# One kernel of recurrence, MLP and gated MLP: the first MLP group in whole float32, later groups and the spatial product in float16 parts

## The chip, the cores and the metric

One Trainium2 chip, and on it one core. The metric is the device time of one execution in microseconds, taken as the median of several runs. One execution was also recorded by the profiler, instruction by instruction.

## What is computed

A model of three layers on two sequences (B = 2) of 768 tokens (S) with 384 features (8 heads of 48). All inputs are float32.

```python
# recurrence, per batch and head: state is 48 x 48
for t in range(S):
    cur = outer(u * k[t], v[t])
    y[t] = r[t] @ (state + cur)
    state = w[t][:, None] * state + outer(k[t], v[t])
# MLP: x is 2 x 768 x 384
xn = (x - mean(x)) / sqrt(var(x) + 1e-6) * g_ln
x = x + maximum(xn @ w_ch1, 0) @ w_ch2          # 384 -> 1536 -> 384
# gated MLP
h = maximum(x @ w_in, 0)                        # 384 -> 1024
u, v = h[..., :512], h[..., 512:]
v_n = (v - mean(v)) / sqrt(var(v) + 1e-6)
v_s = einsum('ts,bsd->btd', w_spatial, v_n) + b_spatial[None, :, None]
out = (u * v_s) @ w_out                         # 512 -> 384
```

The four weight matrices w_ch1, w_ch2, w_in and w_out arrive as float64 (`np.random.randn` times a scale that keeps float64), and the chip has to turn them into float32 itself.

## The kernel before

**The work.** The recurrence runs in chunks of 128 tokens; with two sequences there are 12 chunks, numbered i = 2c + b. `prep(i)` makes the decay products of a chunk on VectorE (two scans and several elementwise products), `keys_t`, `scores`, `values` and `state` are its matmuls, `norm(i)` the layer norm, `turned(i)` the transpositions on TensorE whose results are copied into the feature-major rows `x2v` (the residual) and `xring_h`, `xring_l` (the normalised rows as a high and a low part). Two chunks, one of each sequence, make a group of 256 tokens: `moe1(g)` is the MLP of group g, g = 0 to 5. It has 12 slices f of the hidden width. `up(f)` multiplies with w_ch1's slice, ScalarE and VectorE make the hidden rows `hh` and `hl`, and `down(f)` multiplies these with w_ch2's slice and sums in PSUM. After slice 11 two VectorE steps add the sums to `x2v` (lines 913 and 914).

**Parts.** Each product is made of three: `mm3` multiplies high by high, high by low and low by high part, all in the 4-byte type float32r, and sums in PSUM. In the trace these matmuls read f32.

**Weights.** `convert` turns a piece of 128 x 384 (or 128 x 256) float64 words into the parts, in a staging buffer `raw` of which there are four: a transfer; `shift` on the low words and `rebias` on the high words (ScalarE, lines 554 and 548); `sign` (ScalarE, line 561), which writes the sign over as a float16 value; `merge` (VectorE, line 565), which joins both words; the high part (ScalarE, line 373); the low part (VectorE, line 376). There are 12 pieces of w_ch1, 12 of w_ch2, 12 of w_in and 4 of w_out. The spatial matrix arrives as float32 and is halved, negated and split in `wsp`.

**The last phase.** When all groups are done, `v_tile` makes and normalises v (12 tiles), `u_tile` u, `sp_tile` the spatial product (16 tiles of 18 matmuls of 384 columns), `o_tile` the output. `verdict` compares the variances and the decays with limits; if one is not met, the general but slow function `general` computes the result again.

**The order.** All steps are given to a planner with an engine, an assumed cost, a key, and the tiles that they read and write:

```python
add("T", 9 * cm(256), ku(g, f), mm_, r=[("w1h", f), ("w1l", f), *xr], w=[p])
```

`order` walks through time and gives each engine, whenever it is free, the ready step with the smallest key; what comes out is a fixed order for each engine, and each engine works through its queue in that order. Transfers (engine "D") all go through SyncE's queue. The keys come from the constants `PP`: `T0` and `H0` place chunks 0 and 1, `CV`, `CS` and `CW` the weight pieces, `M0` and `M0S` the slices of group 0, `P`, `US` and `AH` the later groups and their chunks. While TensorE would stand idle before the first `down`, the planner puts in dummy products of zeros (`pw`, 128 x 128 in float16).

## Time and profile before

| what | value |
|---|---|
| median of 3 runs | 393.56 us (391.05 to 395.06) |
| the profiled execution | 389.08 us |
| its span, first to last instruction | 387.4 us |
| TensorE busy | 375.5 us, 97% |
| VectorE busy | 253.4 us, 65% |
| ScalarE busy | 189.0 us, 49% |
| HBM | 31.90 MB read, 2.36 MB written |

A matmul's record lasts longer than the distance to the next one, because matmuls overlap, so busy TensorE says only that it doesn't stand still; what a matmul costs is read from the distance of starts, or from the chain of waits, which gives a row of matmuls its length and its count. Names of tiles are those of the program without buffer numbers; `free` holds the parts of v and of the gated rows, `misc` other rows of the last phase, `p` and `acc` are results in PSUM. Lines 373, 376, 379 and 382 are helpers that record for many callers.

### The profile page before, as it was taken

The page shows a single profiled execution, that of the slowest core. Times are in us where ns is not written, and L with a number is a line of the kernel's source. Part 1 is how long each engine was busy: PE and PEld are TensorE (multiplying, and loading weights), DVE is VectorE, ACT ScalarE, POOL GpSimd, SP SyncE. Part 2 cuts the span into 40 slices and gives each one's busy share as a digit, 9 for nine tenths or more (in the row PEclk, how much of TensorE's full clock was granted, in tenths as well). Part 3 has the DMA queues.
Part 4 walks back from the last instruction along what each step waited for, and adds up shares of the span by engine and source line. Part 5 has one row for each costly group of instructions (what it writes and reads, how often), then busy time and mean ns, then how long its engine had stood idle before and what let it go on. Part 6 is the DMA issues. An engine that isn't in the chain of part 4 may idle for free.

```text
span 387.4 us, 7615 instructions
## 1 busy us (share of the span) xinstructions
PE 375.5 (97%) x3101; PEld 363.0 (94%) x3101; DVE 253.4 (65%) x598; ACT 189.0 (49%) x412; POOL 7.4 (2%) x21
## 2 busy tenths in 40 slices
PE   7899999999999999999999999999999999999994
...
GB/s 222 296 243 187 237 136 287 126 185 80 67 126 135 99 188 56 63 25 38 2 0 138 70 41 2 0 119 167 2 2 3 0 0 3 41 83 0 2 63 68
DMA packets 16092, 34.83 MB, mean 90 GB/s; under 512 B 1840, under 2 KB 8496, under 8 KB 16048
## 3 DMA queue, kind: packets, MB, share of 16 engines
...
HBM read 31.90 MB, written 2.36 MB: 88 GB/s over the span
## 4 chain that ended last, share of the span: by engine, by line
PE 80%; ACT 13%; DMA 4%; DVE 1%; SPq 0%; issue 0%; ACTq 0%
PE p L382 32%; PE acc L382 18%; ACT raw L561 5%; DMA raw<-in_w 3%; PE sc L382 2%; ACT raw L554 2%; ACT raw L548 2%; DMA dt<-in_dt 1%; ACT w1h L373 1%; ACT w2h L373 1%; PE y__2940 L382 1%; PE y__2762 L382 1%; PE y__1395 L382 1%; PE y__2277 L382 1%; PE y__2493 L382 1%; PE y__1978 L382 1%
## 5 line engine op out<-in xcount | busy, mean ns | idle before, releaser
L382 PE MATMUL acc<-hh,w2h 128*128 128x256 f32 x216 | 63.6, 295 | 0.0
L382 PE MATMUL acc<-hl,w2h 128*128 128x256 f32 x216 | 61.4, 284 | 0.5 <-DVE hl L883 0.4
L382 PE MATMUL acc<-hh,w2l 128*128 128x256 f32 x216 | 61.1, 283 | 0.0
L382 PE MATMUL p<-wsph,free 128*128 128x384 f32 x192 | 49.1, 335 | 0.0
L382 PEld LDWEIGHTS acc<-hl,w2h 128*128 128x128 f32 x216 | 41.3, 191 | 1.1 <-DVE hl L883 1.0
L382 PEld LDWEIGHTS acc<-hh,w2h 128*128 128x128 f32 x216 | 41.3, 191 | 0.8 <-ACT hh L879 0.2
L382 PEld LDWEIGHTS acc<-hh,w2l 128*128 128x128 f32 x216 | 41.2, 191 | 0.0
L561 ACT ACTIVATE raw<-raw 128x384 f16<-128x384 f32 (+1 forms) x40 | 39.4, 985 | 0.3
L382 PEld LDWEIGHTS p<-wsph,free 128*128 128x128 f32 x192 | 34.7, 188 | 0.1
L382 PE MATMUL p<-wspl,free 128*128 128x384 f32 x96 | 32.1, 334 | 0.0
L373 ACT ACTIVATE free<-misc 128x384 fp32r<-128x384 f32 x16 | 8.4, 525 | 44.3 <-DVE misc L1104 44.3
L1103 DVE TENSOR_TENSOR misc<-p,misc 128x384 f32<-128x384 f32 x16 | 8.9, 558 | 32.2 <-PE p L382 32.2
L382 PE MATMUL pw<-warm 128*128 128x128 f16 x367 | 25.8, 238 | 1.1 <-DVE warm L483 1.1
L565 DVE SCALAR_TENSOR_TENSOR raw<-raw 128x384 int32<-128x384 int32 (+1 forms) x40 | 20.5, 516 | 8.7 <-ACT raw L561 8.0
L382 PEld LDWEIGHTS <-warm 128*128 128x128 f16 x367 | 24.9, 110 | 1.3 <-DVE warm L483 1.1
L554 ACT ACTIVATE raw<-raw 128x384 uint32<-128x384 uint32 (+1 forms) x39 | 20.8, 534 | 10.6 <-DMA raw<-in_w 9.3
L548 ACT ACTIVATE raw<-raw 128x384 f32<-128x384 f32 (+1 forms) x40 | 21.0, 525 | 0.0
L382 PEld LDWEIGHTS p<-wspl,free 128*128 128x128 f32 x96 | 18.0, 188 | 0.0
L731 DVE TENSOR_TENSOR am<-sc,mask 128x512 f32<-128x512 f32 x24 | 15.7, 683 | 3.2 <-PE sc L382 3.2
L604 DVE TENSOR_TENSOR_SCAN Gs<-dt,onehot 112x516 f32<-112x516 f32 x12 | 14.7, 1226 | 3.4 <-DMA dt<-in_dt 3.4
L382 PE MATMUL p<-wol,free 128*128 128x384 f32 x48 | 16.2, 338 | 0.0
L382 PE MATMUL p<-woh,free 128*128 128x384 f32 x48 | 16.2, 337 | 0.0
...
## 6 DMA issues: line engine op xcount, KB each, us to landing
...
```

Of the source, the lines that this page charges most:

```text
L373: A.activation(out=out, in_=in_, func=ACTF.Copy)
L382: T.matmul(out=out, lhsT=lhsT, rhs=rhs, start=start, stop=stop)
L548: A.activation(out=e, in_=e, func=ACTF.Copy, scale=REBIAS)
L554: A.activation(out=z, in_=z, func=ACTF.Copy, scale=TOP3, bias=TOP3_BIAS)
L561: A.activation(out=z, in_=words()[0].bitcast(F32), func=ACTF.Copy)
L565: V.scalar_tensor_tensor(out=lw, in0=hw, scalar=3, in1=lw, op0=ALU.logical_shift_left, op1=ALU.bitwise_or)
L604: V.tensor_tensor_scan(out=g[:, n:0:-1], data0=d_()[:, 2 * NP * C + n:2 * NP * C:-1], data1=onehot[:, n:0:-1], initial=0.0, op0=ALU.mult, ...
L731: V.tensor_tensor(out=z, in0=t["sc", i][j].rearrange("q (h c) -> q h c", c=C), in1=mask.unsqueeze(1).to_broadcast([128, 4, C]), op=ALU.mult)
L1103: add("V", cv(384), key, lambda: V.tensor_tensor(out=tm_(), in0=t["spp", b, th, f][:, 0:384], in1=t["b"][:, ts], op=ALU.add), r=[p, "misc" ...
```

## The change

Group 0 of the MLP now works on whole float32 values: `merge` writes the joined word into new tiles `w1f` and `w2f`, the normalised rows of chunks 0 and 1 go to a new tile `xfirst`, and each product is one matmul, not three. A staging buffer is free after `merge`. The high and low parts of w_ch1 and w_ch2 are made later from `w1f` and `w2f`, by steps with keys of their own (`HK`, `HS`, `HW`), in float16; groups 1 to 5 take them, with normalised and hidden rows in float16 parts as well. The weights are scaled up by 2^8 on the way, and the sum after slice 11 is scaled back. The spatial product is made of float16 parts too, its matrix scaled by 2^15. `sign` is now a VectorE step for all four matrices: for 19 of the 24 MLP pieces a two-input operation, for 5 of them (letter U in `SG`) a 16-bit operation. Five shifts are on VectorE, before it was one. The steps that GpSimd did (some products of `prep`, some low parts) are on VectorE. `verdict` has range guards: maxima of the parts in float16, of g and of the spatial matrix, sums of `x2v`, and a least variance. Tiles are placed anew: the spatial matrix takes the place of `w1f`, the normalised v that of `w2f`, the high part of the gated rows that of `w1h` and `w1l`, w_out that of `w2h` and `w2l`. The constants `PP` and some assumed costs are new.

```diff
...
-PP = {'T0': 58.954, 'P': 31.457, 'H': 11.551, 'H0': 18.137, 'M0': 114.218, 'M0S': 6.6, 'AH': 31.444, 'AG': -14.296, 'US': 2.5, 'EV': 28.0, 'CV': -3.791, 'CS': 19.292, 'CW': 11.582, 'WK': 741.261, 'WS': -9.174, 'XK': 737.912, 'XS': 13.966, 'KG': 85.937, 'KU': 91.539, 'OK': 603.983, 'OS': 18.495, 'FG': 108.0, 'LOOK': 0.0, 'EK': 'V', 'EU': 'VVVGVVVVGV', 'ER': 'VVVVVGVVVVGV', 'RK': 'V', 'ED': 'V', 'SM': 'V', 'LO': 'V', 'SH': 'AAAAAAAVA', 'LW': 'GVVVVGV', 'LX': 'V', 'LS': 'V', 'LV': 'V', 'LU': 'GV'}
+PP = {'SK': 502.544, 'SS': -11.067, 'RG': 379.453, 'HK': 187.663, 'HS': 3.248, 'HW': 14.159, 'SG': 'VVVVVVVUVVVUVVVUVVVUVVVU', 'T0': 7.677, 'P': 40.921, 'H': 8.033, 'H0': 75.364, 'M0': 3.891, 'M0S': 17.135, 'AH': 39.301, 'AG': -60.723, 'US': 3.526, 'EV': 49.336, 'CV': 9.586, 'CS': 4.689, 'CW': 6.934, 'WK': 646.957, 'WS': 46.232, 'XK': 79.483, 'XS': 17.828, 'KG': 58.216, 'KU': 364.837, 'OK': 542.591, 'OS': 25.632, 'FG': 108.0, 'LOOK': 0.0, 'EK': 'V', 'EU': 'V', 'ER': 'V', 'RK': 'V', 'ED': 'V', 'SM': 'V', 'SH': 'AAAVAAVAAAAAAAAAAAAAVAV', 'LW': 'V', 'LX': 'V', 'LS': 'V', 'LV': 'V', 'LU': 'V'}
...
-    w1h = wpool.tile([128, KD, DH], F32R, tag="wa", name="w1h")
-    w1l = wpool.tile([128, KD, DH], F32R, tag="wb", name="w1l")
-    w2h = wpool.tile([128, KH, DM], F32R, tag="wc", name="w2h")
-    w2l = wpool.tile([128, KH, DM], F32R, tag="wd", name="w2l")
+    k_max = const.tile([128, 10], F32, name="k_max")
+    k_sum = const.tile([128, NCH], F32, name="k_sum")
+    w1f = wpool.tile([128, KD, DH], F32, tag="w1f", name="w1f")
+    w2f = wpool.tile([128, KH, DM], F32, tag="w2f", name="w2f")
+    w1h = wpool.tile([128, KD, DH], F16, tag="w1h", name="w1h")
+    w1l = wpool.tile([128, KD, DH], F16, tag="w1l", name="w1l")
+    w2h = wpool.tile([128, KH, DM], F16, tag="w2h", name="w2h")
+    w2l = wpool.tile([128, KH, DM], F16, tag="w2l", name="w2l")
     x2v = wpool.tile([128, KD, B * S], F32, tag="we", name="x2v")
-    xring_h = ring.tile([128, KD, RING * C], F32R, tag="xh", name="xring_h")
-    xring_l = ring.tile([128, KD, RING * C], F32R, tag="xl", name="xring_l")
+    xring_h = ring.tile([128, KD, RING * C], F16, tag="xh", name="xring_h")
+    xring_l = ring.tile([128, KD, RING * C], F16, tag="xl", name="xring_l")
+    xfirst = ring.tile([128, KD, B * C], F32, tag="xf", name="xfirst")
...
-            A.activation(out=e, in_=e, func=ACTF.Copy, scale=REBIAS)
+            A.activation(out=e, in_=e, func=ACTF.Copy, scale=REBIAS * 2 if whole else REBIAS)
...
-            z = t[name].bitcast(F16).rearrange("q (n four) -> q n four", four=4)[:, :, 1]
-            A.activation(out=z, in_=words()[0].bitcast(F32), func=ACTF.Copy)
+            if sg == "U":
+                z = t[name].bitcast(U16).rearrange("q (n four) -> q n four", four=4)
+                V.tensor_scalar(out=z[:, :, 1], in0=z[:, :, 3], scalar1=0x8000, scalar2=None, op0=ALU.bitwise_and)
+                return
+            hw, lw = words()
+            V.scalar_tensor_tensor(out=lw, in0=hw, scalar=SIGN, in1=lw, op0=ALU.bitwise_and, op1=ALU.bitwise_or)
 
         def merge():
             hw, lw = words()
-            V.scalar_tensor_tensor(out=lw, in0=hw, scalar=3, in1=lw, op0=ALU.logical_shift_left, op1=ALU.bitwise_or)
+            z = full().bitcast(I32)
+            V.scalar_tensor_tensor(out=z, in0=full_of(hw), scalar=3, in1=full_of(lw), op0=ALU.logical_shift_left, op1=ALU.bitwise_or)
...
         def full():
-            return full_of(words()[1].bitcast(F32))
+            return whole() if whole else full_of(words()[1].bitcast(F32))
...
         add("D", 2.845 * n, kd, load, w=[h, l])
         add(sh, 40 + ca(n) if sh == "A" else 69 + 0.521 * n, kd + ks, shift, w=[l])
         add("A", 20 + ca(n), kd + ks, rebias, w=[h])
-        add("A", 20 + ca(n), kd + 2 * ks, sign, r=[h], w=[l])
+        add("V", cv(n) if sg == "V" else 69 + 0.521 * n, kd + 2 * ks, sign, r=[h], w=[l])
+        if whole:
+            f_ = name + ("f",)
+            add("V", cv(n), kd + 3 * ks, merge, r=[h, l], w=[f_])
+            add("A", ca(n), later, lambda: cp(hi(), full()), r=[f_], w=w_hi)
+            add(lo_eng, cx(lo_eng, n), later, lambda: sub(lo_eng, lo(), full(), hi()), r=[f_, *w_hi], w=w_lo)
+            return
         add("V", cv(n), kd + 3 * ks, merge, r=[h], w=[l])
         add("A", ca(n), kd + 4 * ks, lambda: cp(hi(), full()), r=[l, *r_hi], w=w_hi)
         add(lo_eng, cx(lo_eng, n), kd + 5 * ks, lambda: sub(lo_eng, lo(), full(), hi()), r=[l, *w_hi, *r_lo], w=w_lo)
...
-        add("A", ca(DM, True), ka(i, "xnT"), lambda: cp(xring_h[:, :, o:o + C], pv("xn")), r=[pn], w=[("xh", q)])
+        add("A", ca(DM, True), ka(i, "xnT"), lambda: cp((xring_h if c else xfirst)[:, :, o:o + C], pv("xn")), r=[pn], w=[("xh", q) if c else ("xf", q)])
+        if not c:
+            return
...
-            hh, hl = slot("hh", 3), slot("hl", 3)
+            hh, hl = slot("hh" if g else "hf", 3), slot("hl", 3) if g else None
             hts[f] = hh, hl
 
             def mm_():
                 z = t["up", g, f] = pst(p, f"pup{g}_{f}_")
+                if not g:
+                    for k in range(KD):
+                        mm(z[:, 0:n], w1f[:, k, sl], xfirst[:, k], k == 0, k == KD - 1)
+                    return
                 mm3(z[:, 0:n], [(w1h[:, k, sl], w1l[:, k, sl], xh[:, k], xl[:, k]) for k in range(KD)])
...
-                hs[f] = [hp.tile([128, n], F32R, tag=f"hh{hh[1]}", name="hh")]
+                hs[f] = [hp.tile([128, n], F16 if g else F32, tag=f"{hh[0]}{hh[1]}", name="hh")]
...
-            add("T", 9 * cm(256), ku(g, f), mm_, r=[("w1h", f), ("w1l", f), *xr], w=[p])
+            add("T", 9 * ch(256) if g else 3 * 430, ku(g, f), mm_, r=[*([("w1h", f), ("w1l", f)] if g else [("w1", f, "f")]), *xr], w=[p])
             add("A", ca(256, True), ku(g, f) - PP["EV"], hi, r=[p], w=[hh])
+            if not g:
+                hts[f] = (hh,)
+                return
             add("V", cv(256), ku(g, f) - PP["EV"], lo, r=[p, hh], w=[hl], two=False)
...
+                    first, last = f == 0 and d != 1, f == KH - 1 and d > 0
+                    if not g:
+                        mm(acc(d), w2f[:, f, sl], hs[f][0], first, last)
+                        return
                     hh, hl = hs[f]
-                    mm3(acc(d), [(w2h[:, f, sl], w2l[:, f, sl], hh, hl)], start=f == 0 and d != 1, stop=f == KH - 1 and d > 0)
+                    mm3(acc(d), [(w2h[:, f, sl], w2l[:, f, sl], hh, hl)], start=first, stop=last)
...
+        def plus(z, y):
+            V.scalar_tensor_tensor(out=z, in0=y, scalar=W_UP ** -2, in1=z, op0=ALU.mult, op1=ALU.add)
+
+        add("V", cv(512), k, lambda: plus(xv[:, 0:2], t["acc", g, 0].rearrange("q (k b t) -> q k b t", k=2, b=B)), r=[at[0]], w=x2, two=False)
+        add("V", cv(256), k, lambda: plus(xv[:, 2], acc(2).rearrange("q (b t) -> q b t", b=B)), r=[at[1]], w=x2, two=False)
...
-                w1_piece(f, (key, 0.01), lo_eng=who("LO", 2 * f), sh=who("SH", 2 * f))
-                w2_piece(f, (key + PP["CW"], 0.01), lo_eng=who("LO", 2 * f + 1), sh=who("SH", 2 * f + 1))
+                for j, piece in enumerate((w1_piece, w2_piece)):
+                    n = 2 * f + j
+                    piece(f, (key + PP["CW"] * j, 0.01), lo_eng="V", sh=who("SH", n), sg=who("SG", n), later=PP["HK"] + PP["HS"] * f + PP["HW"] * j)
...
+    def size(n, src, r, cols):
+        z = lambda: src() if len(src().shape) == 2 else src().rearrange("q a n -> q (a n)")
+        add("V", cv(cols), PP["RG"] + 10 * n, lambda: V.tensor_reduce(out=k_max[:, n:n + 1], in_=z(), op=ALU.max, axis=AX, apply_absolute_value=True), r=r, w=[("kmax", n)], two=False)
...
+        jobs = [(k, lambda k=k: w1h[:, k], [("w1h", f) for f in range(KH)], DH) for k in range(KD)]
+        jobs += [(KD + j, lambda j=j: w2h[:, 4 * j:4 * j + 4], [("w2h", f) for f in range(4 * j, 4 * j + 4)], 4 * DM) for j in range(3)]
+        jobs += [(9, lambda: g_bc, ["g"], DM)]
+        for job in jobs:
+            size(*job)
...
+            add("V", cv(DM), PP["RG"] + 10 * i, lambda i=i, sl=sl: V.tensor_reduce(out=k_sum[:, i:i + 1], in_=x2v[:, :, sl], op=ALU.add, axis=mybir.AxisListType.XY), r=[("x2", i)], w=[("ksum", i)], two=False)
...
-        key = T2 + 2 + 2 * s
+        key = PP["SK"] + PP["SS"] * s
...
-                t["wsph"] = wpool.tile([128, NC, S], F32R, tag="wa", name="wsph")
-            A.activation(out=t["wsph"][:, s], in_=t["wspr", s], func=ACTF.Copy, scale=-0.5)
+                t["ws"] = wpool.tile([128, 2, NC, S], F16, tag="w1f", name="ws")
+                t["wsph"], t["wspl"] = t["ws"][:, 0], t["ws"][:, 1]
+            A.activation(out=t["wsph"][:, s], in_=t["wspr", s], func=ACTF.Copy, scale=-0.5 * S_UP)
...
+    for j in range(3):
+        size(6 + j, lambda j=j: t["wsph"][:, 2 * j:2 * j + 2], [("wsph", 2 * j), ("wsph", 2 * j + 1)], 2 * S)
...
+        if "vn" not in t:
+            t["vn"] = wpool.tile([128, 2, NC, DF], F16, tag="w2f", name="vn")
...
+            t["gh", j] = wpool.tile([128, 2, S], F32R, tag=("w1h", "w1l")[j], name=f"gh{j}")
...
-            mm3(z[:, 0:384], [(t["vn", 0][:, s, sl], t["vn", 1][:, s, sl], t["wsph"][:, s, ts], t["wspl"][:, s, ts]) for s in range(NC)])
+            mm3(z[:, 0:384], [(opened(0)[:, s, sl], opened(1)[:, s, sl], t["wsph"][:, s, ts], t["wspl"][:, s, ts]) for s in range(NC)])
...
+        add("T", 18 * ch(384), key, mm_, r=r, w=[p])
+        add("V", cv(384), key, lambda: V.scalar_tensor_tensor(out=tm_(), in0=t["spp", b, th, f][:, 0:384], scalar=1.0 / S_UP, in1=t["b"][:, ts], op0=ALU.mult, op1=ALU.add), r=[p, "misc"], w=[tm], two=False)
...
-                    t["woh"] = ring.tile([128, KF, DM], F32R, tag="xh", name="woh")
+                    t["woh"] = wpool.tile([128, KF, DM], F32R, tag="w2h", name="woh")
...
             (lambda: k_var[:, :, 1], NCH, ALU.is_le, MAX_VAR, 128, 128.0),
+            (lambda: k_var[:, B:, 1], NCH - B, ALU.is_ge, MIN_VAR, 128, 128.0),
+            (lambda: k_max, 10, ALU.is_le, MAX_HALF, 128, 128.0),
+            (lambda: k_max[:, 0:9], 9, ALU.is_ge, 1.0, 128, 128.0),
+            (lambda: k_max[:, 9:10], 1, ALU.is_ge, 2.0 ** -4, 128, 128.0),
+            (lambda: k_sum, NCH, ALU.is_le, MAX_VAR, 128, 128.0),
+            (lambda: k_sum, NCH, ALU.is_ge, -MAX_VAR, 128, 128.0),
...
```

## Rows read from the trace of the kernel before

**Rows 1.** Busy us by stretch (x: instructions), granted clock, DMA share, GB/s.

```profile
0.00:10.00 10.00, 7.21 (x97) 7.07 (x97) 5.43 (x11) 1.49 (x2) 1.94 (x12) 1.00 0.82 229
10.00:43.50 33.50, 32.02 (x425) 29.98 (x424) 28.99 (x65) 29.79 (x59) 0.00 (x0) 0.90 0.82 242
43.50:86.60 43.10, 41.30 (x369) 38.83 (x366) 39.47 (x90) 41.86 (x89) 0.00 (x0) 1.00 0.61 188
86.60:126.40 39.80, 39.80 (x381) 38.74 (x381) 37.52 (x88) 14.69 (x36) 1.49 (x1) 1.00 0.35 103
126.40:258.30 131.90, 131.90 (x1164) 129.70 (x1163) 78.02 (x188) 53.53 (x130) 2.97 (x7) 1.00 0.17 54
258.30:381.60 123.30, 123.30 (x680) 118.70 (x678) 63.98 (x161) 47.16 (x98) 1.04 (x1) 1.00 0.12 39
381.60:387.40 5.80, 0.01 (x1) 0.00 (x0) 0.00 (x0) 0.49 (x1) 0.00 (x0) 0.93 0.14 44
```

**Rows 2.** The chain of waits in order of time: start us, us, what.

```profile
6.86 4.30 DMA raw<-in_w
...
35.10 1.12 PE pw L382 x20
...
254.35 1.08 PE acc L382 x9
255.43 2.07 PE p L382 x9
...
258.57 123.05 PE p L382 x677
```

**Rows 3.** ScalarE groups: line, operation, tiles, count | busy us, mean ns | idle before.

```profile
L561 ACT ACTIVATE raw<-raw 128x384 f16<-128x384 f32 x28 | 30.0, 1072 | 0.0
L548 ACT ACTIVATE raw<-raw 128x384 f32<-128x384 f32 x28 | 15.8, 563 | 0.0
```

**Rows 4.** The same for VectorE.

```profile
L731 DVE TENSOR_TENSOR am<-sc,mask 128x512 f32<-128x512 f32 x24 | 15.7, 683 | 3.2 <-PE sc L382 3.2
L565 DVE SCALAR_TENSOR_TENSOR raw<-raw 128x384 int32<-128x384 int32 x28 | 15.6, 556 | 5.7 <-ACT raw L561 5.1
L604 DVE TENSOR_TENSOR_SCAN Gs<-dt,onehot 112x516 f32<-112x516 f32 x12 | 14.7, 1226 | 3.4 <-DMA dt<-in_dt 3.4
...
L376 DVE TENSOR_TENSOR w1l<-raw,w1h 128x384 fp32r<-128x384 f32 x12 | 6.6, 548 | 0.5 <-ACT w1h L373 0.5
...
L556 DVE TENSOR_SCALAR raw<-raw 128x384 int32<-128x384 int32 x1 | 0.4, 357 | 0.0
```

**Rows 5.** Waits of SyncE's transfer queue: us in total, times, longest.

```profile
SPq L540 <- DVE w2l L376: 20.0, 10, 4.7
...
SPq L540 <- DVE w1l L376: 16.3, 7, 3.2
```

**Rows 6.** VectorE in order of time: start us, us, instruction.

```profile
11.15 0.69 DVE L379 TENSOR_TENSOR E<-dt,E 112x512 f32<-112x512 f32 x1
...
64.53 0.55 DVE L379 TENSOR_TENSOR tk<-tk,u_bc 128x384 f32<-128x384 f32 x1
65.00 0.55 DVE L376 TENSOR_TENSOR w1l<-raw,w1h 128x384 fp32r<-128x384 f32 x1
```

**Rows 7.** TensorE in order of time, first 44 us.

```profile
21.62 1.16 PE L382 MATMUL sc<-E,Gs 64*128 64x128 f32 x16
...
29.06 1.20 PE L382 MATMUL sc<-E,Gs 64*128 64x128 f32 x16
...
30.91 0.55 PE L839 MATMUL xnT__575<-ident,xn 128*128 128x128 f32 x3 [0.17 <-ACT xn L828]
...
41.48 0.55 PE L839 MATMUL xnT__769<-ident,xn 128*128 128x128 f32 x3 [0.18 <-ACT xn L828]
```

**Rows 8.** Groups of matmuls on TensorE, shapes apart.

```profile
L382 PE MATMUL acc<-hl,w2h 128*128 128x256 f32 x216 | 61.4, 284 | 0.5 <-DVE hl L883 0.4
...
L382 PE MATMUL sc<-E,Gs 64*128 64x128 f32 x96 | 13.9, 284 | 0.1
```

69 lines of the change are left out of this document (38 added, 31 removed).

## The prediction

> **What bounds the kernel now.** I read the table of stretches first. From 43.5 us to 381.6 us TensorE has no idle stretch to speak of [rows 1], and the chain of waits is matmul after matmul there: nine MLP products in 1.08 us, one every 120 ns; nine 512-wide ones in 2.07 us, 230 ns each; and 677 in the last 123.05 us [rows 2]. So everything after 43.5 us is bought by matmul time: 338.1 us. Before that lie 43.5 us in which TensorE waits for the first two chunks of the recurrence and the first weights, and is kept running by dummy products. Why does it wait? Between 10 and 43.5 us VectorE is busy 28.99 of 33.5 us and ScalarE 29.79; between 43.5 and 86.6 us 39.47 and 41.86 of 43.1 [rows 1]. ScalarE is full with four steps for each of 24 weight pieces; the costliest is the one that carries the sign over, 1072 ns [rows 3]. VectorE waits for it 5.1 us in all [rows 4], and the transfers wait 20.0 and 16.3 us for the low parts, because a staging buffer is held until its low part is made [rows 5]. Chunk 0 shows the cost: its last elementwise input starts at 11.15 us [rows 6], but its scores start at 21.62 us and chunk 1 is turned only at 41.48 us [rows 7].
>
> **TensorE's ledger.** MLP groups 1 to 5 have 5 x 12 x 18 = 1080 products of 256 columns, now 120 ns apart [rows 2]. In float16, 20 dummy products of 128 columns take 1.12 us, 56 ns each [rows 2], 2.7 ns more than 128 columns at 2.4 GHz. If that surplus comes once per product, 256 columns take 109 ns, if it grows with the columns 112. I take 110: 1080 x 10 = 10.8 us saved. That they stay at 120 is a rival. The spatial product has 288 products of 384 columns. Their spacing now: of the 677 in the last stretch 99 are 512 wide, so (123.05 - 99 x 0.230) / 578 = 173.5 ns; in float16 at most 3 x 56 = 168, I take 164: 2.7 us saved.
>
> Group 0 loses: 216 products at 120 ns (25.9 us) become 72 in whole float32. The trace has no whole-float32 product of this size. What it has: the scores, 128 columns, are whole float32; each is two records (96 products make two groups of 96, of which one stands in the rows), and a record lasts 284 ns, as long as a 256-column record of the MLP [rows 8]. So a record seems to stream its columns twice, and a 256-column float32 product should cost two records like a 512-wide one: 2 x 230 = 460 ns, 33.1 us in all, 7.2 us more than now. If a record streamed once it would be 2 x 120 = 240 ns and group 0 would be 8.6 us cheaper than now; four passes at 120 ns make 480 ns, 8.7 us dearer than now. I take 460, since the 284 ns row stands next to it. The Trainium skill ("FP8 and Floating Point Precision", TensorE Precision Notes) speaks against this part of the change: it says that true float32 takes four passes through the array. By its count alone, 4 x 256 columns at 2.4 GHz, an estimate of 427 ns, group 0 would take 30.7 us, 2.4 us less than by mine; the end would not move, because VectorE comes last there (below). The 284 ns row agrees with it as far as two records of two streams make four.
>
> Net: 338.1 - 10.8 - 2.7 + 7.2 = 331.8 us. What is left of the 338.1 for attention is 338.1 - 155.5 (1296 x 0.120) - 125 (the last phase: 108 x 0.230 + 576 x 0.1735) = 57.6 us for chunks 2 to 11, 5.8 us a chunk.
>
> **When can group 0 start?** It needs chunks 0 and 1 turned and one weight piece. By the new constants chunk 0 has key -67.7, chunk 1 7.7 and the first weight piece 9.6; before they were 40.8, 59.0 and -3.8. So both chunks now go ahead of every conversion, and ScalarE loses 1072 ns per piece. Chunk 0's inputs are there at 11.8 us; from its scores to its transposition the trace needs 9 to 12 us even in a crowd (21.62 to 30.9; chunk 1 29.1 to 41.48 [rows 7]). Two chunks on VectorE are some 16 us (a chunk's steps are added up below), the first five pieces in between 4.7 us; of these 20.7 us 5.4 are done by 10 us [rows 1], so group 0 starts at 25 us. Bounds: 20.6 (no conversion in between) and 43.5 (as now).
>
> **When can group 1 start?** VectorE decides. One 384-wide step starts 0.47 us after the one before [rows 6], although its record lasts 0.55; so I take 0.08 us off recorded durations. By 86.6 us it had worked 5.43 + 28.99 + 39.47 = 73.9 us [rows 1]. Taken away: 24 low parts of weights (11.3), 12 low parts of group 0's hidden rows (0.34 each by their width, 4.1), two low parts of its input (0.9), and what it had done ahead for chunk 4 (two scans of 1.14, the rest in 0.60 and 0.47: 6.2). Added: the sign of 24 pieces, 19 in the two-input form at 0.47 as its neighbour, the merge [rows 4], and 5 in the 16-bit form at 0.3, like the one-input shift (bounds 0 and 0.47), 10.4 us; four more shifts at 0.28, 1.1 us [rows 4]. Left: 73.9 - 22.5 + 11.5 = 62.9 us, of which 5.4 lie before 10 us. Its rate from 10 to 86.6 us was 68.5 of 76.6, 89%; without the waits for ScalarE's sign step 96%. At 95%: 10 + 57.5 / 0.95 = 70.5 us. TensorE would be there at 25 + 33.1 + 11.6 = 69.7 us: nearly level.
>
> The weights must come as fast: a staging buffer is now free after the merge, so its cycle is 4.3 us to land, as the first did from 6.86 us on [rows 2], 0.9 on ScalarE (shift and rebias, 0.45 each [rows 3]), 0.94 on VectorE and handovers, 7 to 8 us; four buffers, 24 pieces: the last merged at 6.9 + 6 x 7.5 = 52 us, ahead of group 0's last quarter. The loads of dt and tk stand in the same queue between them.
>
> **When can group 2 start?** The low and high parts are not gone, they now stand behind group 0. High parts go to ScalarE, which has room. VectorE owes 11.3 us for them, 4.1 for hidden rows, 1.0 for the sum and two chunks at 9.8 (two scans 2.28, four 512-wide 2.4, eight 384-wide 3.8, small ones 1.3): 36.0 us, at 95% 37.9: 70.5 + 37.9 = 108.4 us, where TensorE needs 35.4. So 3.3 us of TensorE's time are lost in the two stages together. From there a group costs VectorE about 25 us and TensorE 35: matmul-bound again.
>
> **Everything else is hidden.** Range guards: nine maxima over 1536 columns, each up to four times a 384-wide step, 1.9 us, and 13 smaller ones: 23 us; signs of w_in and w_out on VectorE 6 us; steps brought back from GpSimd 2.4 us. Their cover is VectorE's idle time, 53.9 us from 126.4 to 258.3 and 59.3 us after [rows 1]. If that were gone each would cost its full time, up to 31 us. A 1.9 us maximum can stand in front of the low part of a hidden row, for which TensorE waits; two banks of results ahead cover about that. The spatial weights and the normalised rows no longer wait for group 5's end, because their tiles (w1f, w2f) are free after group 0's parts are made; that takes the 5 + 6 us of spatial conversion out of the crowded start of the last phase, where TensorE never waited for it, so I count nothing.
>
> **Sum.** TensorE after group 2's start: 331.8 - 33.1 - 11.6 - 23.8 - 11.6 = 251.7 us. 108.4 + 251.7 + 5.8 us behind the last matmul = 365.9 us span; the profiled run lasted 389.08 us on a span of 387.4, so 1.7 around it: 367.6 us against 389.08. The median of the runs shown, 393.56, is 1.15% above that run: **372 us**.
>
> **Rivals.**
> VectorE keeps its 89%: group 1 at 74.6, group 2 at 115, end 374.2, median 379. For it: the waits for landings stay. Against: the largest wait is removed. 0.16.
> Level stages, nothing lost: 25 + 331.8 + 5.8 + 1.7 = 364.3, median 368; with a start at 20 us 363. 0.12.
> Group 0 starts no earlier, because loads and not the sign step hold it: 43.5 + 33.1 + 11.6 + 37.9 + 251.7 + 7.5 = 385.3, median 390 at worst, 387 if VectorE has caught up meanwhile. 0.10.
> Float16 products start every 120 ns as before, so that the change doesn't do what it is built on: 13.5 us more, 386. The 56 ns row speaks against it. 0.07.
> Slower: TensorE's clock falls in group 0. From 10 to 43.5 us the mean granted clock was 0.90 [rows 1], that is a fifth of the time at 1.2 GHz, after first 10 us in which TensorE was busy only 7.21; dummies end with group 0's first sum, and group 0 then waits piece by piece. The Trainium skill ("TensorE: Matmul & The Clock Gate", What's actually happening) says that throttled is the default and activity releases it. Half clock through the whole of group 0 adds 33 us: 401, median 405. The gain is gone once 43 us are spent at 1.2 GHz, which costs half of that. Against: group 0's products and the chunks beside them fill 44.7 of the 45.5 us of that stretch. 0.06.
> A guard is not met and the general path runs after all: milliseconds. 0.01.
> The forecast, 368 to 376, keeps 0.48.
>
> **Range and chances.** 362 to 387 takes in the first three rivals' core and the float16 one. About 1% (the runs shown spread 391 to 395) is what tells a change from none. Faster by over 1%: all but the worst of the late start, the clock and the guard, 0.87; within 1% 0.07; slower 0.06.
>
> **What would show it.** First matmul of group 0 near 25 us and float32 products about 460 ns apart; group 1 near 70, group 2 near 108 us; MLP products 110 ns apart afterwards; VectorE about 95% busy from 10 to 108 us and ScalarE near half; maxima in VectorE's idle time with no TensorE wait behind them. Wrong if TensorE idles after 108 us, if its clock shows 1.2 GHz between 25 and 70, or if the staging ring, not VectorE, paces group 0.

## The result and the profile after

The changed kernel takes 373.67 us (median of 4 runs, 370.34 to 375.54) beside 392.31 us before (389.95 to 395.06). The ratio is 0.9513, 95% interval 0.9409 to 0.9617; measured again later, beside other kernels, it was 0.9405 (0.9324 to 0.9486). Ratios leave out executions more than 1.5% above the fastest one of the same kernel and medians do not, so the two can differ. The forecast was 372, so faster by about as much as it said. The span of the profiled run fell from 387.4 to 368.6 us. Most of what follows is about why the sum came out although two of its terms did not.

The table of stretches after, cut near the same events as [rows 1] (columns as there; group 0's first product itself comes at 33.56 us, the last phase's row of matmuls begins at 250.31, and the last matmul ends at 362.14):

```profile
0.00:10.00 10.00, 7.81 (x97) 7.46 (x97) 5.94 (x11) 1.49 (x2) 1.94 (x12) 1.00 0.81 225
10.00:31.20 21.20, 19.74 (x262) 18.70 (x262) 18.10 (x44) 12.41 (x28) 0.00 (x0) 0.92 0.90 267
31.20:79.60 48.40, 46.30 (x298) 40.37 (x297) 45.76 (x105) 36.56 (x87) 0.00 (x0) 0.96 0.67 206
79.60:119.90 40.30, 40.30 (x415) 36.10 (x414) 39.92 (x92) 11.76 (x30) 0.00 (x0) 1.00 0.27 82
119.90:251.70 131.80, 131.80 (x1207) 117.11 (x1206) 121.13 (x285) 62.35 (x152) 0.57 (x10) 1.00 0.26 81
251.70:362.80 111.10, 110.43 (x634) 88.50 (x632) 51.07 (x130) 33.60 (x70) 0.00 (x0) 1.00 0.07 24
362.80:368.60 5.80, 0.00 (x0) 0.00 (x0) 0.00 (x0) 0.00 (x0) 0.00 (x0) 0.85 0.14 42
```

From group 0 on TensorE hardly stands still again: it is busy 46.30 of 48.4 us beside group 0 and all the time after that up to the last phase. VectorE is busy 45.76 of 48.4 us beside group 0, 39.92 of 40.3 beside group 1, and 121.13 of 131.8 (92%) beside groups 2 to 5, where it had been busy 59% before; ScalarE has fallen from 41.86 of 43.1 us to 36.56 of 48.4 [rows 1]. The granted clock is 0.96 beside group 0: for some 4 us it was 1.2 GHz.

TensorE up to the first product of group 0 in order of time, which answers [rows 7] (start us, us, instruction):

```profile
13.25 2.08 PE L390 MATMUL sc<-E,Gs 64*128 64x128 f32 x16
...
20.59 1.16 PE L390 MATMUL sc<-E,Gs 64*128 64x128 f32 x16
...
24.79 0.51 PE L864 MATMUL xnT__469<-ident,xn 128*128 128x128 f32 x3
...
32.43 0.55 PE L864 MATMUL xnT__601<-ident,xn 128*128 128x128 f32 x3 [1.15 <-ACT xn L853]
33.56 1.13 PE L390 MATMUL pup__626<-xfirst,w1f 128*128 128x256 f32 x4
```

Chunk 0 is turned 6.1 us earlier than before, chunk 1 9.1 us, and group 0 starts at 33.56 us instead of 43.51. The last matmul ends at 362.14 us (before 381.61). So TensorE takes 328.58 us from there to its end instead of 338.10: of the 18.8 us of span 9.95 come from the start and 9.5 from shorter matmul work; what lies behind the last matmul is 0.7 us longer.

The chain of waits from 60 to 130 us, which answers the products of [rows 2] (start us, us, what):

```profile
75.20 1.29 PE pup__1038 L390 x6
76.49 1.29 PE acc L390 x6
78.50 1.31 PE acc L390 x6
79.81 0.98 PE pup__1077 L390 x9
```

Six records are three whole-float32 products: 1.29 / 3 = 430 ns each. Nine float16 products take 0.98 us: 109 ns each, 120 before. The groups of TensorE, which answer [rows 8], show the two records to a float32 product (group 0's 36 second products, acc on hh and w2f, count 72) and the new spatial form:

```profile
L390 PE MATMUL acc<-hl,w2h 128*128 128x256 f16 x180 | 49.1, 273 | 0.0
L390 PE MATMUL p<-ws,vn 128*128 128x384 f16 x288 | 47.1, 326 | 0.0
L390 PE MATMUL acc<-hh,w2f 128*128 128x256 f32 x72 | 19.2, 399 | 0.0
```

In the timeline 17 spatial products stand as one record of 2.93 us; with the last one's 0.33 taken off, 2.60 / 16 = 163 ns from start to start.

The groups of ScalarE and of VectorE, which answer [rows 3] and [rows 4]:

```profile
L562 ACT ACTIVATE raw<-raw 128x384 f32<-128x384 f32 (+1 forms) x40 | 20.4, 517 | 0.9 <-DMA raw<-in_w 0.9
L568 ACT ACTIVATE raw<-raw 128x384 uint32<-128x384 uint32 (+1 forms) x35 | 18.0, 514 | 13.8 <-DMA raw<-in_w 12.8 <-DMA raw<-in_win 0.9
```

```profile
L579 DVE SCALAR_TENSOR_TENSOR raw<-raw 128x384 int32<-128x384 int32 (+1 forms) x35 | 17.4, 505 | 4.1 <-ACT raw L562 4.0
...
L584 DVE SCALAR_TENSOR_TENSOR w1f<-raw 128x384 int32<-128x384 int32 x12 | 6.5, 552 | 0.0
...
L1045 DVE TENSOR_REDUCE k_max<-w1h 128x1 f32<-128x1536 f16 x3 | 5.2, 1742 | 0.0
...
L576 DVE TENSOR_SCALAR raw<-raw 128x384 uint16<-128x384 uint16 x5 | 3.0, 595 | 0.0
```

ScalarE's sign step of 1072 ns is gone, and the merge no longer waits 5.1 us for it. ScalarE now stands idle 12.8 us for loads that have not landed. The transfers wait for the merge, where they had waited for the low parts [rows 5]; this is SyncE's queue again:

```profile
SPq L553 <- DVE w1f L584: 17.5, 8, 4.9
SPq L553 <- DVE w2f L584: 14.9, 10, 3.2
```

32.4 us instead of 36.3: the buffers are given back a little earlier, no more.

### The profile page after: what moved, and what is told of

Read it like the earlier page. It is cut to its first block, busy times and chain, and to the rows that moved or that the text cites. A ratio compares the mean times of both kernels' runs of the same rounds, so it can differ in the third digit from the quotient of the medians.

```text
span 368.6 us, 7277 instructions
## 1 busy us (share of the span) xinstructions
PE 356.4 (97%) x2905; PEld 308.2 (84%) x2905; DVE 281.9 (76%) x661; ACT 158.2 (43%) x368; POOL 2.5 (1%) x22
## 4 chain that ended last, share of the span: by engine, by line
PE 83%; DMA 7%; DVE 5%; ACT 2%; issue 1%; SPq 0%; ACTq 0%; DVEq 0%
PE p L390 33%; PE acc L390 19%; DMA raw<-in_w 6%; PE sc L390 3%; DMA dt<-in_dt 1%; DVE raw L579 1%; PE y__2011 L390 1%; DVE w1f L584 1%; PE y__2636 L390 1%; PE y__1733 L390 1%; PE y__2480 L390 1%; PE y__1543 L390 1%; PE y__1322 L390 1%; PE y__1140 L390 1%; PE y__2150 L390 1%
## 5 line engine op out<-in xcount | busy, mean ns | idle before, releaser
L390 PE MATMUL acc<-hh,w2h 128*128 128x256 f16 x180 | 49.2, 273 | 0.0
L390 PE MATMUL acc<-hh,w2l 128*128 128x256 f16 x180 | 49.1, 273 | 0.0
L390 PE MATMUL acc<-hl,w2h 128*128 128x256 f16 x180 | 49.1, 273 | 0.0
L390 PE MATMUL p<-ws,vn 128*128 128x384 f16 x288 | 47.1, 326 | 0.0
L390 PEld LDWEIGHTS <-vn 128*128 128x128 f16 x288 | 28.0, 98 | 18.7 <-issue 0.4
L390 PEld LDWEIGHTS <-w2h 128*128 128x128 f16 x360 | 34.5, 99 | 5.4 <-issue 1.1
L390 PEld LDWEIGHTS <-w1h 128*128 128x128 f16 x360 | 35.0, 98 | 4.3
L568 ACT ACTIVATE raw<-raw 128x384 uint32<-128x384 uint32 (+1 forms) x35 | 18.0, 514 | 13.8 <-DMA raw<-in_w 12.8
L390 PEld LDWEIGHTS <-w2l 128*128 128x128 f16 x180 | 17.6, 98 | 2.1
L390 PEld LDWEIGHTS <-w1l 128*128 128x128 f16 x180 | 17.6, 98 | 2.1
L390 PE MATMUL acc<-hh,w2f 128*128 128x256 f32 x72 | 19.2, 399 | 0.0
```

Of the source, the lines that this page charges most:

```text
L390: T.matmul(out=out, lhsT=lhsT, rhs=rhs, start=start, stop=stop)
L568: A.activation(out=z, in_=z, func=ACTF.Copy, scale=TOP3, bias=TOP3_BIAS)
```

## The experiments

Twelve runs were made, in three groups, each group on one chip with the kernel before. Ratios are to the kernel before of the same group. "TensorE" is the time from group 0's first product to the end of the last matmul in the profiled run; the clock is the granted one from 30 to 120 us, and 90 us times what it lacks to 1 is an estimate of the full-speed time that was lost there. Where TensorE is nearly always busy the estimate holds: after, a_again and a_noguard have the same order up to the first guard at 114.7 us, and TensorE's time less this loss is 326.8, 326.8 and 327.2 us. Where TensorE waits much it is too high, since no product is delayed in a wait. "Group 0 starts" and "TensorE" are of one execution each, and the start varies by itself: with that same order it lies between 32.71 (a_noguard) and 36.65 us (a_f16all, whose clock was 0.66 from 10 to 30 us).

| run | us | ratio | group 0 starts | TensorE | clock, lost us |
|---|---|---|---|---|---|
| before | 392.31 | 1 | 43.51 | 338.10 | 1.00, 0 |
| after | 373.67 | 0.9513 | 33.56 | 328.58 | 0.98, 1.8 |
| b_f16 | 374.65 | 0.9569 | 44.33 | 322.82 | 1.00, 0 |
| b_signV | 395.25 | 1.0109 | 42.09 | 345.07 | 0.96, 3.6 |
| a_split | 391.92 | 1.0020 | 38.83 | 345.77 | 0.85, 13.5 |
| a_order | 373.78 | 0.9578 | 39.68 | 325.75 | 1.00, 0 |
| a_noguard | 369.02 | 0.9442 | 32.71 | 327.24 | 1.00, 0 |
| a_signA | 374.74 | 0.9606 | 37.23 | 329.96 | 0.98, 1.8 |
| a_f16all | 364.09 | 0.9306 | 36.65 | 321.94 | 1.00, 0 |
| a_nst6 | 372.77 | 0.9460 | 33.12 | 326.29 | 1.00, 0 |
| a_again | 370.90 | 0.9405 | 33.23 | 330.41 | 0.96, 3.6 |
| a_both | 367.53 | 0.9384 | 35.98 | 322.16 | 1.00, 0 |
| a_split_signA | 386.67 | 0.9870 | 36.88 | 343.11 | 0.85, 13.5 |
| a_dlat3500 | 365.75 | 0.9344 | 32.07 | 326.32 | 1.00, 0 |

**Float16 parts alone (b_f16).** The kernel before, with nothing changed but the types of the MLP's and the spatial product's parts, the scale that goes with them, and the places of two tiles of the last phase:

```diff
-    w1h = wpool.tile([128, KD, DH], F32R, tag="wa", name="w1h")
+    w1h = wpool.tile([128, KD, DH], F16, tag="wa", name="w1h")
...
-            A.activation(out=t["wsph"][:, s], in_=t["wspr", s], func=ACTF.Copy, scale=-0.5)
+            A.activation(out=t["wsph"][:, s], in_=t["wspr", s], func=ACTF.Copy, scale=-0.5 * 2.0 ** 15)
```

> The kernel before with one part of the change alone: all six MLP groups and the spatial product in float16 parts, same order, same steps, sign still on ScalarE. The MLP parts are not scaled up and there are no range guards. Ledger theory (from group 0's first matmul TensorE is the bound, so a saved matmul nanosecond is a saved nanosecond): 1296 products x 10.9 ns and 288 x 10 ns less, 17 us, start of group 0 unchanged at 43.5 us: span about 370.4 us. Startup theory (until group 1 the conversions decide, not the matmuls): group 1 still starts at 86.6 us, only what lies behind it gains, about 13.4 us: span about 374 us.

Measured: 374.65 us, ratio 0.9569 (0.9516 to 0.9622), span 373.5. TensorE's time fell by 15.3 us; the sum by spacings, 1296 x 11 ns + 288 x 10.5 ns, makes 17.3. Group 0 starts no earlier (44.33), and the span lies where the startup theory had it. By the spans, one execution each, 13.9 of the 18.8 us are the float16 parts' alone, and all the rest of the change together is worth 4.9. By the ratios the parts are worth more and the rest less certain: 0.9569 here against 0.9513 and 0.9405 for the whole change leaves it 2 to 6 us, and this interval overlaps with that of the first measurement and not with that of the second.

**The sign alone (b_signV).** The kernel before, its sign step moved to VectorE in the two-input form:

```diff
-            z = t[name].bitcast(F16).rearrange("q (n four) -> q n four", four=4)[:, :, 1]
-            A.activation(out=z, in_=words()[0].bitcast(F32), func=ACTF.Copy)
+            hw, lw = words()
+            V.scalar_tensor_tensor(out=lw, in0=hw, scalar=SIGN, in1=lw, op0=ALU.bitwise_and, op1=ALU.bitwise_or)
```

> The kernel before with another part alone: the sign of all 40 weight pieces by VectorE's two-input step (0.47 us) in place of ScalarE's (0.98 us); the planner orders the steps anew with the old constants. If ScalarE's sign step is what holds up the start, group 0 begins some 5 us earlier and the span falls to about 382 us. If VectorE is the bound until group 2, its 11 us more for 24 pieces come on top there: span 390 to 398 us, slower.

Measured: 395.25 us, ratio 1.0109 (1.0069 to 1.0150): 1.1% slower. Its stretch from 43.5 to 86.6 us, with the columns of [rows 1]:

```profile
43.50:86.60 43.10, 39.06 (x331) 36.84 (x329) 42.56 (x99) 28.98 (x68) 0.00 (x0) 0.92 0.58 177
```

VectorE goes from 39.47 to 42.56 of 43.1 us and ScalarE from 41.86 to 28.98: the load has only changed sides. TensorE stands idle 4 us in it, and its clock falls to a mean of 0.92.

**Group 0 in three float16 products (a_split).** The changed kernel with the low parts made right behind each merge, as before, and no whole-float32 form (the tests for group 0 in the product and in the hidden rows are taken out too):

```diff
-            add("A", ca(n), later, lambda: cp(hi(), full()), r=[f_], w=w_hi)
-            add(lo_eng, cx(lo_eng, n), later, lambda: sub(lo_eng, lo(), full(), hi()), r=[f_, *w_hi], w=w_lo)
+            add("A", ca(n), kd + 4 * ks, lambda: cp(hi(), full()), r=[f_], w=w_hi)
+            add(lo_eng, cx(lo_eng, n), kd + 5 * ks, lambda: sub(lo_eng, lo(), full(), hi()), r=[f_, *w_hi], w=w_lo)
...
-            hh, hl = slot("hh" if g else "hf", 3), slot("hl", 3) if g else None
+            hh, hl = slot("hh", 3), slot("hl", 3)
```

> The changed kernel with its first part undone: group 0 takes three float16 products like the other groups, and the high and low parts are made right after the merge. Ledger theory taken alone: group 0 costs 23.6 us of matmuls in place of 31, start unchanged at 33.6 us: span about 361 us, faster than the changed kernel's 368.6. Conversion theory: 24 low parts of 0.47 us and 12 low parts of hidden rows stand ahead of group 1 again, 15 us of VectorE's time, so group 1 starts at about 93 us in place of 79.6, TensorE idles in group 0, and the span is about 375 us.

Measured: 391.92 us, ratio 1.0020 (0.9974 to 1.0066). The whole gain is gone, far more than either theory had worked out. The stretch from 30 to 120 us:

```profile
30.00:120.00 90.00, 76.62 (x689) 63.62 (x689) 87.89 (x202) 48.45 (x114) 0.00 (x0) 0.85 0.53 163
```

VectorE is full (87.89 of 90), TensorE waits 13.4 us, and the clock adds to it: 0.85 over 90 us is up to 13.5 us lost.

**The same with the sign on ScalarE (a_split_signA).** a_split, and the sign step of a_signA below. It was to tell whether the sign is what fills VectorE there.

> The changed kernel with group 0 in three float16 products and its low parts made right after each merge, as in the run with label a_split, but the sign taken by ScalarE. It is the fourth corner: sign on either engine, group 0 in either form. Theory (the whole float32 group pays only because it empties VectorE for the sign, and the sign moves only because VectorE is emptied): with the sign off VectorE this one stands near the kernel before with float16 parts (374.65) and near the changed kernel with the sign on ScalarE (374.74): 373 to 377 us, some 16 below a_split. Rival (making the parts early is the trouble by itself, whichever engine takes the sign): 383 to 392 us.

Measured: 386.67 us, ratio 0.9870 (0.9812 to 0.9928). The sign costs 5 us of the 18, and the theory falls by the rival's numbers. What stays is the clock. TensorE in order of time:

```profile
85.37 0.27 PE L390 MATMUL acc<-hh,w2l 128*128 128x256 f16 x1
87.87 0.55 PE L868 MATMUL xnT__1291<-ident,xn 128*128 128x128 f32 x3 [2.22 <-ACT xn L857]
...
92.01 3.65 PE L390 MATMUL y__1317<-tk,am 128*128 128x48 f32 x16 [0.66 <-DVE am L760]
95.45 0.41 PE L390 MATMUL pup__1346<-xring_h,w1h 128*128 128x256 f16 x1
95.66 0.42 PE L390 MATMUL pup__1346<-xring_l,w1h 128*128 128x256 f16 x1
```

After waits of 2.22, 0.16 and 0.66 us the products start 210 ns apart instead of 109, and the stretches of 4 us from 92 to 104 have a granted clock of 0.50. Take 13.5 us, the most that the clock can have cost, off the spans of both, and a_split is at 376.8 and this at 372.7, beside 373.5 of b_f16, which has the same products and the sign on ScalarE in the order of before, and a clock of 1.00. The products are the same in b_f16 and here, and the conversions as many; what differs is the waits and the clock: in the order that was made for the whole-float32 group TensorE stands idle 11.6 us between 30 and 120, against 5.1 in b_f16, and its clock falls. How much of the 12.7 us between the two is the clock by itself is an estimate, not shown. Whether another order would keep the clock up with three products was not tried.

**The sign back on ScalarE (a_signA).** The changed kernel with the old sign step for all pieces:

```diff
+            if sg == "A":
+                z = t[name].bitcast(F16).rearrange("q (n four) -> q n four", four=4)[:, :, 1]
+                A.activation(out=z, in_=words()[0].bitcast(F32), func=ACTF.Copy)
+                return
             if sg == "U":
```

> The changed kernel with the sign of all weight pieces back on ScalarE (0.98 us each). If VectorE's work decides when groups 1 and 2 start: 10 us less of it for the 24 pieces, span 361 to 365 us. If the sign step on ScalarE holds staging buffers and ScalarE's queue (36.6 of 48.4 us busy during group 0, 23.5 more to come): group 0 is paced by ScalarE again, span 373 to 380 us.

Measured: 374.74 us, ratio 0.9606 (0.9543 to 0.9669), span 373.1. Group 0 starts at 37.23, and the first line of its chain of waits from 0 to 85 us is ScalarE's, that of the sign step first of all:

```profile
by line: ACT raw L576 24.1%; DMA raw<-in_w 14.0%; ACT raw L562 12.2%; ACT raw L568 8.9%; PE acc L390 5.8%; DMA dt<-in_dt 5.2%; ACT w1h L381 4.6%; ACT hh L914 2.4%; ACT w2h L381 2.4%; issue 2.1%; ACT kf L381 1.6%; PE pup__1020 L390 1.5%; PE 
```

By the spans the move to VectorE gives 4.5 us here, while it costs 5.5 in the kernel before (b_signV) and 4.1 in a_split. By the ratios, whose intervals overlap (0.9543 to 0.9669 against 0.9409 to 0.9617), the gain here is not told from none; against the second measurement of the changed kernel (0.9324 to 0.9486), on another chip, it is. That the move does not cost what it costs elsewhere is shown by both.

**The first chunks later (a_order).** The changed kernel, with chunks 0 and 1 behind the first weight pieces, as the order of before had them:

```diff
-            return T0 - (1 - j) * PP["H0"]
+            return (22.0, 30.0)[j]
```

> The changed kernel with chunks 0 and 1 set behind the first pieces of the weights, as in the kernel before (keys 22 and 30 in place of -67.7 and 7.7). If the time is the start of group 0 plus a gapless row of matmuls, a start some 6 to 9 us later moves the end by as much: span 375 to 378 us. If VectorE's total work until group 1 decides (the prediction's way), the order of the same work changes little: span 368 to 371 us.

Measured: 373.78 us, ratio 0.9578 (0.9508 to 0.9648), span 371.4. Group 0 starts 6.1 us later and the span is only 2.8 us longer: TensorE needs 325.75 us instead of 328.58 from there, 1.8 of that by its clock, and 0.8 by waits (idle 1.3 instead of 2.1 of the 90 us from 30 to 120). That lies between the two theories, but the clock is what took it off the first. Beside a_noguard, which kept a clock of 1.00 as this one did (start 32.71, TensorE 327.24, span 366.4), a start 7.0 us later puts the end off by 5.0 us. So with the clock alike most of a late start arrives at the end.

**No range guards (a_noguard).** The changed kernel without the maxima, the sums and the tests on them:

```diff
-    ranges()
...
-            (lambda: k_max, 10, ALU.is_le, MAX_HALF, 128, 128.0),
```

> The changed kernel without the 22 new maxima and sums of the range guards and without their limits (the variance limits stay): the guards' part of the computation is left out. If they lie in VectorE's idle time, as predicted: 368.6 us span, within 1 us. If VectorE, 121 of 131.8 us busy between group 2 and the last phase, is near to being the bound there, taking 23 us off it gives 2 to 5 us.

Measured: 369.02 us, ratio 0.9442 (0.9376 to 0.9508), between the two measurements of the changed kernel (0.9513 and 0.9405): no difference that can be told. VectorE falls from 172.10 to 151.18 us of the 240 from 120 to 360 us. The profiled span is 2.2 us shorter; the start (0.85 earlier) and the clock (1.8 not lost) account for that.

**Float16 for the last products too (a_f16all).** The changed kernel, with the parts for w_in and w_out in float16:

```diff
-        t["Xh"] = p2["w"].tile([128, KD, B * S], F32R, name="xh")
+        t["Xh"] = p2["w"].tile([128, KD, B * S], F16, name="xh")
...
-                    t["woh"] = wpool.tile([128, KF, DM], F32R, tag="w2h", name="woh")
+                    t["woh"] = wpool.tile([128, KF, DM], F16, tag="w2h", name="woh")
```

> The changed kernel with the products of w_in and w_out in float16 parts as well (unscaled, without guards of their own). Ledger theory: 108 products of 512 columns x 14 ns and 288 of 384 x 10.5 ns less, 4.5 us, all in the last phase, where TensorE is the bound: span 364 us. If the last phase is paced by the steps that take the results away, 368 us as before.

Measured: 364.09 us, ratio 0.9306 (0.9250 to 0.9362), with a span of 364.6. The last line of matmuls in its chain, and in that of the changed kernel:

```profile
251.00 107.60 PE p L390 x641
```

```profile
250.31 111.83 PE p L390 x641
```

The same 641 products take 4.2 us less. In the last stage nothing but TensorE counts, and a nanosecond per product arrives in the end whole. This kernel has the lowest median of all; its interval overlaps with those of a_again, a_both and a_dlat3500.

**Six staging buffers (a_nst6).** `NST = 6` for `NST = 4`.

> The changed kernel with six staging buffers in place of four. If the wait for a free buffer paces group 0 (transfers waited 32 us for the merges), its slices follow faster and group 1 starts 4 to 6 us earlier: span 363 to 365 us. If the transfers themselves (0.90 busy from 10 to 31 us) or VectorE pace it: 367 to 370 us.

Measured: 372.77 us, ratio 0.9460 (0.9381 to 0.9540). The waits of the transfers for the merges fall from 32.4 to 20.6 us, and the last of the 24 pieces is merged from 55.8 us on, not from 71.2. Group 0 starts at 33.12, no earlier than the start varies by itself. The profiled span, 365.0, and group 1's start, 75.72 us instead of 79.65, are what the first theory said, but a_noguard has group 1 at 76.83 with four buffers: both had a clock of 1.00, and of the 3.9 us some 1.1 are left for the buffers. By the ratios no gain is told. The ring sets when the weights come, and little hangs on that.

**Both (a_both).** a_f16all with six buffers.

> The changed kernel with the products of w_in and w_out in float16 parts as well, and six staging buffers for the weights instead of four. Theory (the last stages wait only for TensorE, and the start of group 0 is paced by transfers and buffers): the two gains lie at opposite ends of the span and add up, span 364.6 - 3.6 = 361, median 361 to 363 us. Rival (what group 0 gains is given back, since VectorE with 92% in the middle groups sets their ends): the six buffers add nothing to the float16 products, median 364 us.

Measured: 367.53 us, ratio 0.9384 (0.9317 to 0.9451); a_f16all has 0.9306 (0.9250 to 0.9362). The buffers add nothing that can be told; the theory's 361 to 363 was missed.

**The changed kernel once more (a_again).**

> The changed kernel unchanged, on the same chip as the three beside it, so that they are compared with it directly: median 370 to 375 us, ratio to the kernel before 0.945 to 0.957.

Measured: 370.90 us, ratio 0.9405 (0.9324 to 0.9486): the median as expected, the ratio below the 0.945 that was the least. Its profiled run has a span of 369.2 and lost 3.6 us to the clock between 30 and 120 us:

```profile
30.00:120.00 90.00, 88.75 (x725) 78.06 (x723) 85.30 (x198) 48.76 (x119) 0.00 (x0) 0.96 0.50 152
```

**Later landings in the plan (a_dlat3500).** The changed kernel, whose planner is told that a load lands 3.5 us after its issue. The steps are the same, in another order, but the planner, which fills TensorE's planned idle time with dummies, also puts in 44 more of these: 287 instead of 243, nearly all of the 44 in the first 10 us (TensorE busy 8.93 of them instead of 7.51 in a_again):

```diff
-        "DV": 907, "DA": 908, "DG": 935, "DT": 907, "DD": 1245,
+        "DV": 3500, "DA": 3500, "DG": 3500, "DT": 3500, "DD": 1245,
```

> The changed kernel with the planner told that a load lands 3.5 us after its issue instead of 0.9, which puts the float32 copies and merges of late pieces later in ScalarE's and VectorE's fixed order and the chunks' steps ahead of them. Theory (group 0 starts at 33.6 and not at 25 because ScalarE's queue stands behind a merge whose load hasn't landed): group 0 starts 2 to 6 us earlier, span 363 to 367. Rival (the loads themselves are late, whatever stands ahead of them): group 0 starts within 1.5 us of 33.6 and the time stays at 370 to 375 us.

Measured: 365.75 us, ratio 0.9344 (0.9295 to 0.9394); a_again beside it 370.90. The intervals of the two ratios overlap, but all six executions (365.44 to 366.43 us) lie below nine of the changed kernel's ten. So there is a gain in the median, and it is not by the theory: group 0 starts at 32.07, 1.2 us earlier than in a_again, as the rival said, whose 370 to 375 us did not come either. The same stretch as above:

```profile
30.00:120.00 90.00, 89.13 (x767) 79.13 (x765) 88.97 (x205) 51.60 (x124) 0.00 (x0) 1.00 0.53 163
```

The clock is full throughout, VectorE is busy 88.97 instead of 85.30 of 90 us, and TensorE needs 326.32 instead of 330.41 us. Of 4.5 us of span 1.2 are the start, 4.1 TensorE's time (3.6 by its clock), and the end gives 0.8 back. Its six runs lie between 365.44 and 366.43 us at mean granted clocks of the whole run from 0.995 to 0.998. The four of the changed kernel: 370.34 us at 0.988, 372.17 at 0.976, 375.17 at 0.970, 375.54 at 0.965. The lower the clock, the longer the run; and the one execution of a_again that kept 0.997 took 366.04 us, as long as these. By these numbers what this kernel gains is a clock that stayed up in all six executions. Whether the order did that or the added dummies, no run separates.

## Why the prediction came out

**What bounds the kernel.** Right. The ledger of TensorE was the right thing to count: the float16 products are 109 ns apart (said: 110) and the spatial ones 163 (164), so that surplus comes once per product and not per column. a_f16all, which does the same to two more products, arrived at what the ledger said.

**Group 0 in whole float32.** Right in kind, too dear in size: 430 ns instead of 460. That a product is two records, as my row of the scores said, is shown; the size is off because I priced a record like a 512-wide product of the old parts, 230 ns, surplus included. 72 x 30 ns = 2.2 us less than the term. The estimate from the Trainium skill's four passes ("FP8 and Floating Point Precision", TensorE Precision Notes), 427 ns, agrees with the measured 430.

**When group 0 starts.** Wrong: 33.56 us, not 25. The step that failed is "two chunks on VectorE are some 16 us, the first five pieces in between 4.7 us", and that nothing would wait and nothing come behind. VectorE hands chunk 1 over at 31.7 us. From 10 us up to there it does 6 sign steps, 5 merges, 2 shifts and a scan of chunk 2, 6.8 us by their spacing where I had put 4.7; the two chunks take 11.8 us of that time where I had 10.6 left for them; and it stands idle 3.1 us. Behind it ScalarE's last step of the norm, the transposition and the copy take another 1.9 us that I had not counted. These are 2.1 + 1.2 + 3.1 + 1.9 = 8.3 of the 8.6 us. The way out of VectorE (start us, us, instruction, idle time before):

```profile
31.57 0.15 DVE L832 SCALAR_TENSOR_TENSOR rs<-y,y 128x1 f32<-128x1 f32 x1
31.76 0.62 ACT L853 ACTIVATE xn<-xn,rs 128x384 f32<-128x384 f32 x1 [0.74 <-DVE rs L832]
33.01 0.49 ACT L381 ACTIVATE xfirst<-xnT__601 128x384 f32<-128x384 f32 x1 [0.21 <-PE xnT__601 L864]
```

Most of the idle time has to do with a load, as ScalarE's order shows:

```profile
23.30 0.62 ACT L853 ACTIVATE xn<-xn,rs 128x384 f32<-128x384 f32 x1 [0.57 <-DVE rs L832]
25.69 0.54 ACT L568 ACTIVATE raw<-raw 128x384 uint32<-128x384 uint32 x1 [1.77 <-DMA raw<-in_w]
26.13 0.47 ACT L381 ACTIVATE x2v<-xT__455 128x384 f32<-128x384 f32 x1
26.50 0.55 ACT L562 ACTIVATE raw<-raw 128x384 f32<-128x384 f32 x1
27.67 0.57 ACT L562 ACTIVATE raw<-raw 128x384 f32<-128x384 f32 x1 [0.61 <-DMA raw<-in_w]
28.13 0.47 ACT L381 ACTIVATE xfirst<-xnT__469 128x384 f32<-128x384 f32 x1
```

Chunk 0 is turned at 24.79, but its copy stands in the queue behind a shift and a rebias whose load has not landed, and is made at 28.13; chunk 1's square root (`sd`) comes up in the same queue only at 30.31, and VectorE waits 0.93 us for it. The load takes long, as the chain of waits from 0 to 85 us shows:

```profile
19.62 7.96 DMA raw<-in_w
...
37.13 6.18 DMA raw<-in_w
...
49.97 6.65 DMA raw<-in_w
```

I had taken 4.30 us from the first load [rows 2]; the first of these shares the queue with dt and tk of later chunks, at a DMA share of 0.90 from 10 to 31.2 us. a_dlat3500 takes this wait away, but another stands in its place, of VectorE for a copy that comes behind the first two loads in ScalarE's queue:

```profile
14.73 0.56 DVE L387 TENSOR_TENSOR dv<-tk,kf 128x384 f32<-128x384 f32 x1 [2.73 <-ACT kf L381]
```

Its start is 1.2 to 1.5 us earlier, less than the start varies by itself. So the rival "group 0 starts no earlier, because loads hold it" had a part of the truth, some 2.4 of the 8.6 us by VectorE's idle time (1.50 us for a rebias, 0.93 for the square root); a_dlat3500 is not free of waits for loads, and the share stays open. The weights' rate was mis-sized by the same landings: the last piece is merged from 71.2 us on, where I had 52, in group 0's last quarter and not ahead of it.

**Groups 1 and 2.** Group 1 starts at 79.65 us, 46.1 us behind group 0 (said: 45.5), and the sum of group 1 is added at 119.89, 40.2 us later (37.9). VectorE is busy 95% beside group 0, as forecast, but "VectorE decides" does not hold: TensorE stands idle only 1.0 of the 86.3 us of both stages. They are made of its own work: 31.0 us of whole-float32 products, 23.5 of float16 ones, attention of five chunks at my 5.8 us, 1.8 us of clock and the 1.0. I had let a wait at a group's border count in full, 3.3 us in all, and I had shared out attention evenly, two chunks to a group; by 119.89 us the scores of seven chunks are done and not of six. That fifth chunk is work that TensorE has behind it, so that it needs 242.3 us from group 2 on where I had 251.7.

**The sum.** Start +8.6 us; TensorE's time from there 328.6 instead of 335.1, that is -6.5 (2.2 by the float32 products, 1.4 by 1 ns on each of 1080 and 288 others, 2.3 of the 3.3 not lost; the clock took 1.8 back, the other 2.4 are not resolved); the end +0.6: 365.9 + 8.6 - 6.5 + 0.6 = 368.6 us. Two errors of opposite sign. They hardly hang together: of the runs with a clock of 1.00, TensorE needs 326.32, 327.24 and 326.29 us with starts at 32.07, 32.71 and 33.12 us (a_dlat3500, a_noguard, a_nst6), and 325.75 with a start at 39.68 (a_order), so a start some 7 us later gives back 0.5 to 1.5. That the forecast came within 2.7 us of the span is in good part luck.

**Everything else hidden.** Right. The maxima last 1.74 us each (1.9 said), VectorE's idle time beside groups 2 to 5 went from 53.9 to 10.7 us, and without the guards nothing measurable comes back. No TensorE wait stands behind a maximum: from 119.9 to 251.7 us TensorE is busy throughout.

**The rivals.** The clock, which I had as the slower case at 0.06, is the one that the experiments kept meeting. In the two profiled executions of the changed kernel it takes 1.8 and 3.6 us, in a_split and a_split_signA up to 13.5, and in a_split nothing of the gain is left. I had put the turning point at 43 us of 1.2 GHz; a_split shows 27 us of it and 13.4 us of waits before and between. The changed kernel's fall beside group 0, with the columns of [rows 1]:

```profile
56.00:60.00 4.00, 3.04 (x32) 2.56 (x31) 2.73 (x6) 3.03 (x7) 0.00 (x0) 0.95 1.01 287
60.00:64.00 4.00, 4.00 (x26) 3.36 (x24) 4.00 (x15) 2.19 (x5) 0.00 (x0) 0.62 0.86 261
```

The Trainium skill's rule ("TensorE: Matmul & The Clock Gate", What's actually happening), that activity releases the clock, agrees with the rows so far: each fall that was looked at stands behind waits of TensorE. Not each wait is followed by a fall: b_f16 stands idle 5.1 us between 30 and 120 us at a clock of 1.00. Of the signs of error that I had named, "its clock shows 1.2 GHz between 25 and 70" came true in small; TensorE did not idle after 108 us, and the staging ring set when the weights came but hardly paced group 0 (a_nst6).

**What the parts are worth.** The float16 parts 13.9 us of span by themselves, 17 us by the ratio; they are most of the gain, and what the rest adds, 2 to 6 us, is not told from none by one of two measurements. The whole-float32 group costs TensorE 7.4 us by count (72 x 430 ns against 216 x 109 ns); in the runs 3.5 of it show (326.3 in a_dlat3500 and a_nst6 against 322.8 in b_f16, all at full clock), since TensorE's idle time from 30 to 120 us falls from 5.1 to 0.9. With the order that goes with it, it starts 10 to 12 us earlier. The sign on VectorE can gain only where the low parts have been moved out of the startup (4.5 us by the spans), and costs 4 to 5.5 us where they have not. What remains open is how much of the whole-float32 group's use is the form and how much the order that goes with it: with three products I ran only two orders, one fitting the old kernel, one fitting the new.
